# A bias product that reads contiguous columns, with the interleaving moved to the copy out of PSUM

## The chip, the cores and the metric

The kernel runs on one core of a Trainium2 chip. Its engines are TensorE (PE, with its weight loads shown as PEld), VectorE (DVE), ScalarE (ACT), GpSimd (POOL) and SyncE (SP, which issues most DMAs). The metric is the device time of one execution in microseconds; a smaller one is better. The time before is the median of three runs. A difference of under about 1% is hard to tell from no change.

## The reference

Attention over 4 batches, 8 heads, 576 positions and a head size of 64, with a learned bias that depends on the two positions, is followed by a mixture of 8 experts with one expert per token. All is in float32.

```python
scores = scale * np.matmul(q, k.transpose(0, 1, 3, 2))
psi_rel = np.log1p(np.abs(rel))
psi_i = np.log1p(np.maximum(pos[:, None].astype(np.float32), 1.0))
x = (psi_rel / psi_i)[..., None]
h = np.maximum(x @ w1 + b1, 0.0)          # 32 hidden units
bias = h @ w2                              # [576, 576, 8 heads]
scores = scores + bias.transpose(2, 0, 1)[None]
scores = scores - np.max(scores, axis=-1, keepdims=True)
attn = np.exp(scores)
attn = attn / (np.sum(attn, axis=-1, keepdims=True) + 1e-09)
out = np.matmul(attn, v)
...
# tokens [2304, 512]: softmax gate of the best of 8 experts, then
out[mask] = gate_w[mask, None] * (np.maximum(x[mask] @ w1[e], 0.0) @ w2[e])
```

## The kernel before

**Attention.** The work is cut into 80 units. A unit is one head of one pair of batches and one chunk of query rows: chunk c (0 to 3) holds the rows 4p + c with p up to 127, chunk 4 the last 64 rows. The first 40 units belong to the first pair of batches, in the chunk order 4, 0, 1, 2, 3; the second pair repeats the order. A unit (`unit`) runs on PE the scores `s` (L686), on DVE the sum of scores and bias with its minimum (L700), on ACT the exponential (L703), on PE the transposes (L717) into the banks `t0`, `t1` and `m`, on ACT or DVE their copies `pts` (L723), on PE the product with the values (L738) and a last transpose (L743), and on DVE the division (L755).

**The bias.** It is the same for both pairs of batches, so `bias_step` makes it once, in 36 steps (four for chunk 4, eight for each other chunk), between the units of the first pair; most steps have a priority some 13 units ahead of their chunk's first unit. A step covers 16 query rows for all 576 key columns. DVE (seldom POOL or ACT) makes four tiles `hid` of 128 x 576 (L616), each of them 4 rows times 32 hidden units; POOL makes the weights `wt` (L596). PE then multiplies each `hid` by 32 weight columns, and the four products lie side by side in the four column tiles of the array. They go to PSUM in two halves: columns 0 to 255, then columns 256 to 575. Both halves use the one bank `m`, apart from the first steps, which also use `t0`, `t1` and `o`. ACT (seldom DVE) adds a constant and copies each half to the tile `stg` (L644, L648), in pieces of 256, 256 and 64 columns; POOL copies 64 columns to the front (L653) and issues the DMA of `stg` to DRAM (L654). A unit later loads its bias with SP (`bt`, L667).

In `stg`, the first 512 key columns stand in the order c, r (all columns 4r, then all 4r + 1, and so on), since keys are loaded that way. Before the change the product makes this order: PE reads `hid` in steps of four columns (16 bytes), writes the bank in a row, and the copy has both sides contiguous in runs of 64:

```python
... hx[x]()[:, a:a + 256].rearrange("p (r c) -> p c r", c=4) ...   # L629, in steps of 4
... hx[x]()[:, a + 256:a + n] ...                                  # L631, columns 512 to 575
src = m()[:, lo:lo + k].rearrange("p (c r) -> p c r", c=4)         # L640
```

Each float32 product is two instructions in the trace (two passes over its columns), so a step has 16 of 256 columns and 8 of 64.

**The order.** All of attention is given as operations with dependencies, buffers and a priority to a list scheduler (`Sched`) that runs when the program is built and writes every engine's program in one fixed order. Its durations (300 and 440 for the two halves of a product) and the priorities (`oB`, `oO`, `oL`, `BL`, `FINQ`, `WP` and others, in units) are numbers at the head of the file. On the chip each engine goes through its own list in order and waits for semaphores. SP and POOL queue their DMAs in that order too. The tile `hid` has five buffers, `stg` two, `bt` four, `wt` four.

After attention the tokens are sorted to slots by expert and the experts' products run (`moe`); the change doesn't touch that code.

Of the kernel before, what the change touches and what calls it, by code (L numbers as in the profile page):

```python
# [19 lines left out]
B, H, S, D = 4, 8, 576, 64  # L20
# [13 lines left out]
QPE = ((0, 4, 0),)  # L34
EA, EB = 6, 4
NB = NS - EA
PEN, PENP, PACE = 155.677, 2000, 2000
oS, oB, oP, oT, oE, oA, oO, oX, oL = 0.26, -1, -0.817, -0.323, -1, 3.114, -2.843, 1.206, 0.169
BL, BS, QL = 13.245, 0.415, 0.625
FINP, FINQ = 12, 1.278  # L40
FINE, GEP = 1.277, 1
WP, W2P, W1P = 56.805, 56, 70.081
WHP, RLP, XEP, XP = 96.779, 0, -75.386, 5
L1P = [(k, x, r) for k in range(4) for x, r in ((0, 0), (0, 1), (1, 0))]
GL, W0P, W0S = 6.297, -25.544, 4.236
# [210 lines left out]
class Kern:  # L256
# [327 lines left out]
    def bias_step(self, c, g, prio):  # L584

        nc, S = self.nc, self.S
        t0 = c * 32 + g * 4
        tag = ("bias", c, g)
        relu = (c, g) in BACT
        if relu:  # L590

            wts, w = [], lambda x: self.w2bd
        else:
            wt = self.buf("wt", [128, 4, 32], pool="sm_wt")
            wts, w = [wt], lambda x: wt()[:, x]
            S.op([("POOL", 361, lambda: nc.gpsimd.tensor_tensor(wt(), self.w2bd.unsqueeze(1).to_broadcast([128, 4, 32]), self.sall[:, t0 // 4].unsqueeze(2).to_broadcast([128, 4, 32]), ALU.mult))], [], [tag + ("w",)], [wt], prio)  # L596
        hids, hx = [], []
        for x in range(4):
            src, off = (self.L, 499 - 16 * (4 * g + x) - c) if c < 4 else (self.L2, 60 - 4 * (4 * g + x))
            own = BHID.get((c, g))  # L600
            if own is None:
                hid = self.buf("hid", [128, S_])
                hids.append(hid)
            else:

                if x % 2 == 0:
                    big = self.buf("pp", [128, 2 * S_]) if own == "pp" else self.buf("pts", [128, 9, 128], pool="pt")
                    hids.append(big)
                if own == "pp":
                    hid = lambda big=big, x=x: big()[:, S_ * (x % 2):S_ * (x % 2) + S_]  # L610
                else:
                    hid = lambda big=big, x=x: big().rearrange("p a b -> p (a b)")[:, S_ * (x % 2):S_ * (x % 2) + S_]
            hx.append(hid)

            def act(e, hid=hid, src=src, off=off, x=x):
                e.tensor_scalar(hid(), src[:, off:off + S_], self.thr[:, t0 + x:t0 + x + 1], None, ALU.max)  # L616

            def rel(hid=hid, src=src, off=off, x=x):
                nc.scalar.activation(hid(), src[:, off:off + S_], AF.Relu, bias=self.wcol[:, 1:2], scale=self.sall.rearrange("p g t -> p (g t)")[:, t0 + x:t0 + x + 1])

            alts = [("ACT", 667, rel)] if relu else [("DVE", 440, lambda act=act: act(nc.vector)), ("POOL", 1699, lambda act=act: act(nc.gpsimd), PENP)]
            S.op(alts, ["L"] if c < 4 else [], [tag + ("h", x)], [hids[-1]], prio)
        stg = self.buf("stg", [128, 640])
        for k, (a, n) in enumerate(((0, 256), (256, 320))):
            m = self.buf(("t0", "t1", "o", "m")[(2 * g + k) % 4] if c == 4 or c == 0 and g < BBK else "m", [128, 512])

            def mm(a=a, n=n, m=m):
                for x in range(4):
                    nc.tensor.matmul(m()[32 * x:32 * x + 32, 0:256], w(x), hx[x]()[:, a:a + 256].rearrange("p (r c) -> p c r", c=4), start=True, stop=True, tile_position=(0, 32 * x))  # L629
                for x in range(4 if n > 256 else 0):  # L630
                    nc.tensor.matmul(m()[32 * x:32 * x + 32, 256:n], w(x), hx[x]()[:, a + 256:a + n], start=True, stop=True, tile_position=(0, 32 * x))  # L631

            tm = tag + ("m", a)
            S.op([("PE", 300 if n == 256 else 440, mm)], [tag + ("w",)] + [tag + ("h", x) for x in range(4)], [tm], [*wts, m] + hids, prio)

            def ev(e, lo, k, m=m, a=a):
                col = a + lo
                if col < 512:
                    out = stg()[:, 64:576].rearrange("p (c r) -> p c r", c=4)[:, :, col // 4:(col + k) // 4]
                    src = m()[:, lo:lo + k].rearrange("p (c r) -> p c r", c=4)  # L640
                else:
                    out, src = stg()[:, col + 64:col + 64 + k], m()[:, lo:lo + k]
                if e is nc.scalar:
                    e.activation(out, src, AF.Identity, bias=0.0 if relu else self.corr)  # L644
                elif relu:
                    e.tensor_copy(out, src)
                else:
                    e.tensor_scalar(out, src, self.corr, None, ALU.add)  # L648

            for lo, k in ((0, 256), (256, 64))[0:1 if n == 256 else 2]:  # L650
                S.op([("ACT", 144 + 0.833 * k, lambda ev=ev, lo=lo, k=k: ev(nc.scalar, lo, k)), ("DVE", 70 + 1.04 * k, lambda ev=ev, lo=lo, k=k: ev(nc.vector, lo, k), PEN)], [tm] + ([] if relu else ["corr"]), [tag + ("s", lo + a)], [m, stg], prio)
        rows = self.bsc[c].rearrange("i h k -> (i h) k")
        S.op([("POOL", 333, lambda: nc.gpsimd.tensor_copy(stg()[:, 0:64], stg()[:, 576:640]))], [tag + ("s", 512)], [tag + ("t",)], [stg], prio)  # L653
        S.op([("POOL", 1038, lambda: nc.gpsimd.dma_start(rows[128 * g:128 * g + 128, :], stg()))] + ([("SP", 550, lambda: nc.sync.dma_start(rows[128 * g:128 * g + 128, :], stg()), PSB)] if c == 4 or c == 0 else []), [tag + ("t",), tag + ("s", 0), tag + ("s", 256)], [("bsc", c)], [stg], prio, 910)  # L654
# [806 lines left out]
```

## Time and profile before

| | before |
|---|---|
| median of 3 runs | 734.16 us (732.21 to 737.54) |
| the profiled execution | 733.53 us, of which the profile's span is 731.6 us |
| PE busy in the span | 652.0 us (89%) |
| DVE, ACT, POOL busy | 558.2, 466.3, 175.5 us |
| mean granted TensorE clock | 0.97 |
| attention with bias steps | to about 210 us of the span |
| attention without them | 210 to about 410 us |

The profile is one execution. Busy times are unions of the intervals in which the engine had an instruction in flight, so a busy PE includes the tails of its pipeline. The 1.9 us between the span and the execution's time lie outside the profile.

### The profile page before, as it was taken

To read this page: it belongs to the slowest core of one execution; us is meant where nothing else is said; L and a number is where in the kernel's file an instruction comes from. 1 tells how busy PE (TensorE), PEld (TensorE's weight loads), DVE (VectorE), ACT (ScalarE), POOL (GpSimd) and SP (SyncE) were. 2 spreads that over 40 slices of the span, in tenths; PEclk is the share of its full clock that TensorE was granted. 3 is DMA by queue.
4 is the path that set the end of the run, shared out by engine and by line. 5 is a ranking of instruction groups with operands and counts; after the bars stand their busy time and mean duration, and the time that the engine had idled before them with its cause. 6 is when DMAs were issued, how large, how long until landed. Compare 5 with 4: busy or idle time off the path is not lost.

```text
span 731.6 us, 19239 instructions
## 1 busy us (share of the span) xinstructions
PE 652.0 (89%) x6649; PEld 424.6 (58%) x6649; DVE 558.2 (76%) x1579; ACT 466.3 (64%) x1058; POOL 175.5 (24%) x273
## 2 busy tenths in 40 slices
PE   8679999998999979899999965899999998899983
PEld 3345545555467657677776754764674476357541
DVE  5877677788868998898988864869589967978642
ACT  4566567666678888898998434857266546736200
POOL 3545543344221122311201165000000000000163
PEclk9799999999999999999999989999999999999997
DMA  7685544726478966988878669846299459739532
GB/s 233 195 216 173 161 154 135 210 87 164 139 203 196 275 154 129 182 179 201 198 162 188 149 188 215 204 88 186 82 231 191 163 109 222 180 113 188 110 127 99
DMA packets 147908, 124.03 MB, mean 170 GB/s; under 512 B 93830, under 2 KB 122758, under 8 KB 147808
## 3 DMA queue, kind: packets, MB, share of 16 engines
q1 hardware_dynamic: 140400, 97.19, 56.2%
q0 software_dynamic: 7408, 25.52, 10.6%
q8 instruction: 60, 0.98, 0.6%
q14 instruction: 40, 0.33, 0.1%
HBM read 80.70 MB, written 22.29 MB: 141 GB/s over the span
## 4 chain that ended last, share of the span: by engine, by line
issue 37%; PE 27%; DVE 7%; ACT 5%; POOL 4%; DMA 2%; another core or an unknown queue 0%; POOLq 0%; ACTq 0%; DVEq 0%; SPq 0%
PE o L738 8%; PE s L686 6%; PE t L717 5%; PE m L629 4%; ACT pp L703 2%; POOL out L1295 2%; DVE ss L700 2%; DMA mht<-macc 2%; PE o L743 1%; ACT pts L723 1%; PE m L717 1%; DVE khl L513 1%; PE e L1040 1%; DVE pts L723 0%
## 5 line engine op out<-in xcount | busy, mean ns | idle before, releaser
L1290 PE MATMUL p<-w1s,mxt 128*128 (+1 forms) x960 | 126.8, 275 | 4.9 <-DVE macc L1051 3.5
L1290 PE MATMUL p<-w2s,mht 128*128 (+1 forms) x504 | 115.0, 379 | 9.4 <-DVE macc L1382 8.2
L703 ACT ACTIVATE pp<-ss,mx 128x576 f32<-128x576 f32 x144 | 112.7, 787 | 13.5 <-DVE mx L700 12.4
L700 DVE CUSTOM_DVE_ANT_0 ss<-s,bt 128x576 f32<-128x576 f32 x144 | 104.3, 751 | 13.2 <-PE s L686 11.0
L1290 PEld LDWEIGHTS <-mxt 128*128 128x128 f16 (+1 forms) x960 | 93.5, 99 | 31.0 <-issue 4.2
L738 PE MATMUL o<-pts,v 128*64 128x128 f32 x1600 | 105.3, 278 | 2.2 <-DVE xt L755 1.3
L738 PEld LDWEIGHTS o<-pts,v 128*64 128x64 f32 x1600 | 86.1, 136 | 25.5 <-issue 12.9
L1290 PEld LDWEIGHTS <-mht 128*128 128x128 f16 (+1 forms) x504 | 49.0, 99 | 67.5 <-issue 15.2
L616 DVE TENSOR_SCALAR hid<-L,thr 128x576 f32<-128x576 f32 x128 | 65.0, 567 | 29.6 <-PE m L631 29.6
L717 PE MATMUL t<-ident,pp 128*128 128x128 f32 x576 | 85.0, 279 | 2.1 <-ACT pp L703 1.6
L686 PE MATMUL s<-kt,qt 64*128 64x512 f16 (+3 forms) x960 | 75.7, 287 | 4.2 <-DVE mx L700 3.2
L1295 POOL DMA_INDIRECT out<-macc,kept x21 | 21.0, 998 | 239.4 <-DVE macc L1382 235.1
L723 ACT COPY pts<-t 128x512 f32<-128x512 f32 x125 | 70.0, 594 | 11.0 <-PE t L717 9.8
L629 PE MATMUL m<-hid,wt 128*32 128x256 f32 x488 | 68.5, 625 | 8.9 <-ACT stg L644 3.4
L1251 ACT ACTIVATE junk<-raw 128x1024 bf16<-128x1024 f32 x50 | 53.0, 1059 | 31.6 <-DMA raw<-in_moe_w 18.8
L717 PEld LDWEIGHTS t<-ident,pp 128*128 128x128 f32 x576 | 63.8, 141 | 13.1 <-ACT pp L703 4.7
L1344 ACT ACTIVATE h<-p 128x256 f16<-128x256 f32 x78 | 28.5, 384 | 61.9 <-PE p L1290 34.4
L686 PEld LDWEIGHTS <-qt 64*128 64x128 f16 (+1 forms) x960 | 39.3, 97 | 43.9 <-issue 15.5
L644 ACT ACTIVATE stg<-m,corr 128x256 f32<-128x256 f32 (+1 forms) x88 | 33.7, 418 | 46.3 <-PE m L631 24.7
L1382 DVE SCALAR_TENSOR_TENSOR macc<-p,aux,macc 128x512 f32<-128x512 f32 x63 | 46.2, 752 | 21.1 <-PE p L1290 16.1
L1345 DVE SCALAR_TENSOR_TENSOR h<-p,h 128x256 f16<-128x256 f32 x80 | 32.4, 420 | 26.2 <-ACT h L1344 26.2
L1257 DVE SCALAR_TENSOR_TENSOR w1s<-raw,wz,w1s 128x1024 f16<-128x1024 f32 x32 | 40.7, 1278 | 0.1
(335 smaller groups left out, 1063.1 us busy)
## 6 DMA issues: line engine op xcount, KB each, us to landing
raw<-in_moe_w SPq DMA_DIRECT2D x60, 512.0 KB, 4.8
bt<-bsc SPq DMA_DIRECT2D x64, 320.0 KB, 3.5
bsc<-stg POOLq DMA_DIRECT2D x33, 320.0 KB
bt<-bsc SPq DMA_DIRECT2D x32, 160.0 KB, 4.2
xs<-row POOLq DMA_DIRECT2D x16, 256.5 KB
v<-in_v SPq DMA_DIRECT2D x8, 512.0 KB, 5.3
kr<-in_k SPq DMA_DIRECT2D x8, 512.0 KB, 7.8
q<-in_q SPq DMA_DIRECT2D x8, 512.0 KB, 5.5
```

The costliest lines, as they stand in the source:

```text
L616: e.tensor_scalar(hid(), src[:, off:off + S_], self.thr[:, t0 + x:t0 + x + 1], None, ALU.max)
L629: nc.tensor.matmul(m()[32 * x:32 * x + 32, 0:256], w(x), hx[x]()[:, a:a + 256].rearrange("p (r c) -> p c r", c=4), start=True, stop=True, ...
L686: nc.tensor.matmul(out, lq, k, start=xq + xk == 0, stop=xq == 1, tile_position=(64 * b, 0 if c < 4 else 64 * b))
L700: nc.vector.tensor_tensor_reduce(out=sx(), in0=ss[b]()[:, 448 * b:448 * b + S_], in1=bt()[:, 64 - 64 * b:640 - 64 * b], scale=1.0, scalar= ...
L703: nc.scalar.activation(pp()[:, S_ * b:S_ * b + S_], sx(), AF.Exp, bias=mx()[:, b:b + 1], scale=-1.0, accum_out=sums()[:, h, b:b + 1])
L717: nc.tensor.transpose(t()[:, 128 * k:128 * k + 128], pp()[:, lo + 128 * k:lo + 128 * k + 128], self.ident)
L723: (e.copy if e is nc.scalar else e.tensor_copy)(pts()[:, at:at + n].rearrange("p a b -> p (a b)"), t()[:, 0:128 * n])
L738: nc.tensor.matmul(ob()[64 * b:64 * b + 64, k:k + 128], vv[:, 8 + b if j == 4 else 4 * b + j, :], pts()[:, pb, :], start=j == 0, stop=j == ...
L1251: S.op([("ACT", 1230, lambda: nc.scalar.activation(out() if not own else dst(0), rv() if own else raw(), AF.Square, scale=2.0 ** (-8 if wh ...
L1257: S.op([("DVE", 1280, lambda: nc.vector.scalar_tensor_tensor(dst(1), rv(), z(3), dst(0), ALU.mult, ALU.subtract))], [t + (3,), t + (2,)] + ...
L1290: nc.tensor.matmul(out[c, 0:n], lhs[:, c], w[:, bass.ds(ev[s] + at, n)], start=start, stop=stop)
L1382: S.op([("DVE", 750, lambda a=a, r=r, p2=p2: v.scalar_tensor_tensor(a, p2(), r, a, ALU.mult, ALU.add))], [("p2", q, s), ("rs", q)], [("acc ...
```

## The change

The product reads each `hid` in contiguous columns, the first half 256 and the second half all 320 in one matmul, so L631 and its eight instructions a step go. The bank `m` then holds the columns in their natural order, and the copy of each piece of 256 reads PSUM in steps of four elements and writes `stg` in the same runs of 64 as before. The last 64 columns are copied as before. The scheduler's duration of the second half goes from 440 to 390, and numbers that set the order are changed (a table of numbers; its effect on the order is shown behind the diff).

```diff
--- before.py
+++ after.py
@@ -34,12 +34,12 @@
 QPE = ((0, 4, 0),)
 EA, EB = 6, 4
 NB = NS - EA
-PEN, PENP, PACE = 155.677, 2000, 2000
-oS, oB, oP, oT, oE, oA, oO, oX, oL = 0.26, -1, -0.817, -0.323, -1, 3.114, -2.843, 1.206, 0.169
-BL, BS, QL = 13.245, 0.415, 0.625
-FINP, FINQ = 12, 1.278
+PEN, PENP, PACE = 155.677, 2000, 1643.511
+oS, oB, oP, oT, oE, oA, oO, oX, oL = 0.26, -1.529, -0.817, -0.323, -1, 3.114, -3.254, 1.206, 1.584
+BL, BS, QL = 13.929, 0.415, 0.625
+FINP, FINQ = 12, 1.913
 FINE, GEP = 1.277, 1
-WP, W2P, W1P = 56.805, 56, 70.081
+WP, W2P, W1P = 55.887, 56, 70.081
 WHP, RLP, XEP, XP = 96.779, 0, -75.386, 5
 L1P = [(k, x, r) for k in range(4) for x, r in ((0, 0), (0, 1), (1, 0))]
 GL, W0P, W0S = 6.297, -25.544, 4.236
@@ -626,18 +626,16 @@
 
             def mm(a=a, n=n, m=m):
                 for x in range(4):
-                    nc.tensor.matmul(m()[32 * x:32 * x + 32, 0:256], w(x), hx[x]()[:, a:a + 256].rearrange("p (r c) -> p c r", c=4), start=True, stop=True, tile_position=(0, 32 * x))
-                for x in range(4 if n > 256 else 0):
-                    nc.tensor.matmul(m()[32 * x:32 * x + 32, 256:n], w(x), hx[x]()[:, a + 256:a + n], start=True, stop=True, tile_position=(0, 32 * x))
+                    nc.tensor.matmul(m()[32 * x:32 * x + 32, 0:n], w(x), hx[x]()[:, a:a + n], start=True, stop=True, tile_position=(0, 32 * x))
 
             tm = tag + ("m", a)
-            S.op([("PE", 300 if n == 256 else 440, mm)], [tag + ("w",)] + [tag + ("h", x) for x in range(4)], [tm], [*wts, m] + hids, prio)
+            S.op([("PE", 300 if n == 256 else 390, mm)], [tag + ("w",)] + [tag + ("h", x) for x in range(4)], [tm], [*wts, m] + hids, prio)
 
             def ev(e, lo, k, m=m, a=a):
                 col = a + lo
                 if col < 512:
                     out = stg()[:, 64:576].rearrange("p (c r) -> p c r", c=4)[:, :, col // 4:(col + k) // 4]
-                    src = m()[:, lo:lo + k].rearrange("p (c r) -> p c r", c=4)
+                    src = m()[:, lo:lo + k].rearrange("p (r c) -> p c r", c=4)
                 else:
                     out, src = stg()[:, col + 64:col + 64 + k], m()[:, lo:lo + k]
                 if e is nc.scalar:
```

On PE the first bias steps (chunk 4, at the start of the kernel) stand like this before; `o`, `m` and `t` are PSUM banks, `pp`, `pts` and `hid` hold the hidden units, `w2bd` and `wt` are weights, and each row is the four column tiles of one product:

```order
L629 MATMUL o<-pp,w2bd 32x256 x4
L629 MATMUL m<-pp,w2bd 32x256 x4
L631 MATMUL m<-pp,w2bd 32x64 x4
L629 MATMUL t_284<-hid,wt 32x256 x4
L629 MATMUL t_290<-hid,wt 32x256 x4
L631 MATMUL t_290<-hid,wt 32x64 x4
L382 MATMUL m<-bcst 128x1
L629 MATMUL t_318<-pts,wt 32x256 x4
```

and now:

```order
L629 MATMUL o<-pp,w2bd 32x256 x4
L629 MATMUL m<-pp,w2bd 32x320 x4
L629 MATMUL t_280<-hid,wt 32x256 x4
L629 MATMUL t_288<-hid,wt 32x320 x4
L382 MATMUL m<-bcst 128x1
L629 MATMUL t_310<-pts,wt 32x256 x4
```

Every product of 256 and the one of 64 behind it became one of 320; the sequence of the steps is the same.

On ACT one unit in the middle of the stretch with bias steps stands like this before (L644 copies the bias, L703 is the exponential, L742 a small copy for L743, L723 the transposed probabilities):

```order
L703 ACTIVATE pp,sums<-ss,mx 128x576
L742 COPY os<-o 128x128
L644 ACTIVATE stg<-m,corr 128x4x64
L644 ACTIVATE stg<-m,corr 128x64
L723 COPY pts<-t_1860 128x512
L723 COPY pts<-t_1872 128x512
L723 COPY pts<-m 128x128
L703 ACTIVATE pp,sums<-ss,mx 128x576
L644 ACTIVATE stg<-m,corr 128x4x64
```

and now, with line numbers lower by two:

```order
L701 ACTIVATE pp,sums<-ss,mx 128x576
L740 COPY os<-o 128x128
L642 ACTIVATE stg<-m,corr 128x4x64
L642 ACTIVATE stg<-m,corr 128x64
L721 COPY pts<-t_1863 128x512
L721 COPY pts<-t_1877 128x512
L721 COPY pts<-m 128x128
L701 ACTIVATE pp,sums<-ss,mx 128x576
L642 ACTIVATE stg<-m,corr 128x4x64
```

The order within the unit is the same.

On SP, which issues the loads, the part at the first units stands like this before (`bt` is the bias of a unit, read back from the DRAM tile `bsc`; `v`, `q`, `qm`, `kr` are the inputs):

```order
L542 DMA qm<-in_q 64x4x64 x2
L440 DMA v<-in_v 128x4x256
L667 DMA bt<-bsc_197 64x640 x2
L443 DMA v<-in_v 64x4x64
L440 DMA v<-in_v 128x4x256
L324 DMA rcst<-in_rcst 128x293
L325 DMA row<-in_moe_expert_emb 8x512
L667 DMA bt<-bsc_197 64x640 x4
L544 DMA q<-in_q 128x4x256
L582 DMA_TRANSPOSE qt<-qab 128x8x128
L667 DMA bt<-bsc_197 64x640 x2
```

and now:

```order
L542 DMA qm<-in_q 64x4x64 x2
L665 DMA bt<-bsc_197 64x640 x2
L440 DMA v<-in_v 128x4x256
L665 DMA bt<-bsc_197 64x640 x2
L324 DMA rcst<-in_rcst 128x293
L325 DMA row<-in_moe_expert_emb 8x512
L665 DMA bt<-bsc_197 64x640
L443 DMA v<-in_v 64x4x64
L440 DMA v<-in_v 128x4x256
L582 DMA_TRANSPOSE qt<-qab 128x8x128
L665 DMA bt<-bsc_197 64x640 x3
```

Ahead of the second large load of `v` there are now five loads of `bt`, where there were two, and the first load of `q` stands behind the next three instead of ahead of them.

## Rows read from the trace of the kernel before

**Rows 1.** The page: busy time of each engine with its share of the span and its instruction count, and the granted TensorE clock in 40 equal slices of the span (9 is 90% or more of full speed).

```profile
PE 652.0 (89%) x6649; PEld 424.6 (58%) x6649; DVE 558.2 (76%) x1579; ACT 466.3 (64%) x1058; POOL 175.5 (24%) x273
...
PEclk9799999999999999999999989999999999999997
```

**Rows 2.** Busy time by stretch: the stretch in us, its length, then the busy time of PE, PEld, DVE, ACT and POOL (in brackets the instructions), the granted TensorE clock, the share of the DMA engines and GB/s.

```profile
0.00:30.00 30.00, 21.00 (x158) 9.71 (x159) 21.02 (x52) 15.56 (x25) 14.23 (x27) 0.84 0.61 193
30.00:50.00 20.00, 17.15 (x172) 9.06 (x169) 16.15 (x40) 10.58 (x20) 8.85 (x20) 0.90 0.83 242
50.00:60.00 10.00, 8.36 (x99) 4.92 (x96) 8.02 (x24) 8.66 (x21) 6.00 (x9) 1.00 0.80 191
60.00:80.00 20.00, 20.00 (x252) 11.66 (x250) 13.78 (x34) 11.66 (x28) 9.08 (x17) 1.00 0.51 154
80.00:110.00 30.00, 27.23 (x315) 13.85 (x311) 21.55 (x60) 18.73 (x51) 14.57 (x26) 1.00 0.53 170
110.00:170.00 60.00, 58.26 (x677) 33.39 (x673) 44.90 (x115) 42.07 (x116) 25.02 (x43) 1.00 0.48 144
170.00:190.00 20.00, 17.34 (x206) 8.68 (x204) 15.55 (x50) 12.81 (x34) 7.95 (x15) 1.00 0.57 153
190.00:210.00 20.00, 19.98 (x245) 11.93 (x242) 13.34 (x41) 13.66 (x38) 3.54 (x7) 1.00 0.78 195
210.00:410.00 200.00, 186.70 (x2397) 143.02 (x2396) 174.80 (x608) 176.19 (x453) 41.03 (x64) 1.00 0.81 184
```

**Rows 3.** The chain that ended last, in order of time, over one unit of attention and the start of the next: start in us, length in us, engine, tile, line.

```profile
119.75 1.09 PE m L629 x8
120.83 1.24 PE o L738 x20
122.08 1.02 PE m L629 x8
123.10 0.12 PE m L631 x8
123.21 0.58 PE t L717 x4
123.80 0.11 PE o L743
...
124.45 0.84 PE s L686 x12
125.31 1.09 PE m L629 x8
```

**Rows 4.** The timeline of PE in narrow windows between 208.1 and 209.4 us, one half of a bias step at full clock: start, length from the first start to the last end, line, operands, count. A window lists what was in flight in it, so each row of four is one pass of four column tiles.

```profile
208.14 0.64 PE L629 MATMUL m<-hid,wt 128*32 128x256 f32 x4
208.58 0.65 PE L629 MATMUL m<-hid,wt 128*32 128x256 f32 x4
209.03 0.26 PE L631 MATMUL m<-hid,wt 128*32 128x64 f32 x4
209.10 0.24 PE L631 MATMUL m<-hid,wt 128*32 128x64 f32 x4
209.27 0.33 PE L717 MATMUL t<-ident,pp 128*128 128x128 f32 x1
```

**Rows 5.** The same for a bias step on tiles t at 27.8 to 29.9 us: first the row of the busy time by stretch (length, PE busy, granted clock, DMA share, GB/s), then three passes of the timeline.

```profile
27.90:29.90 2.00, 2.00 (x24) 0.50 0.42 114
...
29.19 0.65 PE L629 MATMUL t<-pp,wt 128*32 128x256 f32 x4
29.64 0.30 PE L631 MATMUL t<-pp,wt 128*32 128x64 f32 x4
...
29.72 0.33 PE L631 MATMUL t<-pp,wt 128*32 128x64 f32 x4
```

**Rows 6.** The timeline of DVE and ACT in the unit of rows 3: start, length, line, operands, count, and in square brackets the idle time before with what ended it.

```profile
123.23 1.95 DVE L616 TENSOR_SCALAR hid<-L,thr 128x576 f32<-128x576 f32 x4 [0.78 <-PE m L631]
123.36 0.68 ACT L644 ACTIVATE stg<-m,corr 128x256 f32<-128x256 f32 x2 [0.95 <-PE m L631]
...
123.93 1.07 ACT L723 COPY pts<-t 128x512 f32<-128x512 f32 x2
...
125.03 0.82 ACT L703 ACTIVATE pp<-ss,mx 128x576 f32<-128x576 f32 x1
...
126.59 0.47 ACT L644 ACTIVATE stg<-m,corr 128x256 f32<-128x256 f32 x1 [0.65 <-POOL qs L560]
...
126.97 0.76 ACT L703 ACTIVATE pp<-ss,mx 128x576 f32<-128x576 f32 x1
...
127.72 0.25 ACT L742 COPY os<-o 128x128 f32<-128x128 f32 x1
...
128.93 0.68 ACT L644 ACTIVATE stg<-m,corr 128x256 f32<-128x256 f32 x2 [0.95 <-PE m L631]
```

**Rows 7.** Groups of instructions from 50 to 210 us, each shape apart: line, engine, operation, operands, shapes, count, then busy time in us, mean ns of one, and the idle time before them with what ended it.

```profile
L644 ACT ACTIVATE stg<-m,corr 128x256 f32<-128x256 f32 x55 | 26.1, 475 | 42.9 <-PE m L631 22.0 <-issue 8.8 <-PE m L629 6.9
...
L644 ACT ACTIVATE stg<-m,corr 128x64 f32<-128x64 f32 x28 | 8.6, 307 | 0.0
...
L616 DVE TENSOR_SCALAR hid<-L,thr 128x576 f32<-128x576 f32 x111 | 55.9, 562 | 28.4 <-PE m L631 28.4
...
L629 PE MATMUL m<-hid,wt 128*32 128x256 f32 x448 | 61.3, 625 | 7.6 <-ACT pts L723 3.3 <-ACT stg L644 3.2 <-DVE lgs L862 0.5
```

## The prediction

> **What bounds the kernel now.** I read the page first: PE is busy for 89% of the span [rows 1]. Where a busy engine is also the one waited for differs by stage, so the busy time by stretch comes next. The steps of the bias lie before 210 us. In the 100 us made of 60 to 80, 110 to 170 and 190 to 210, PE is busy for 97 to 100% and DVE and ACT for 58 to 75%; in the 60 us between them (50 to 60, 80 to 110, 170 to 190) PE has 84 to 91% and DVE 72 to 80% [rows 2]. Behind 210 us ACT and DVE have 88 and 87%, so a faster PE gives nothing there.
>
> The chain that ended last then shows what PE does. From 119.75 to 125.31 us it stays on PE without a wait: half a bias step, the product with the values, the other half, transposes, scores, and the next unit's half step [rows 3]. That is 5.56 us for one unit and one bias step. Of it the bias has 1.09 us at the start and 1.13 from 122.08 to 123.21.
>
> What holds up the bias product is in the narrow windows. A pass of four column tiles with 256 columns starts at 208.14, the next at 208.58, the passes of 64 columns at 209.03 and 209.10, the transposes at 209.27 [rows 4]. So 256 columns in steps of four cost 0.44 to 0.45 us a pass, 1.7 ns a column, and 64 contiguous ones 0.07, 1.1 ns a column. [...] Four contiguous streams side by side do run faster per column, which the 64 columns show.
>
> **The change part by part.** *The product.* I need a contiguous pass of 256 and of 320 columns, which the trace lacks. One side: 64 columns in 0.07 to 0.08 us, so 1.25 ns a column at most, 0.32 and 0.40 us. Other side: a float32 transpose, a single tile, reads 128 contiguous columns in 0.11 us [rows 3], 0.86 ns a column, 0.22 and 0.275 us. With 0.86 ns the 64 columns would be 0.055 and leave some 0.015 for starting four tiles; this fits both rows, and I take 0.24 and 0.29 us. First half: two passes, 0.89 before (208.14 to 209.03), 0.48 after, 0.41 saved. Second half: 0.89 and 0.14 for the passes of 64, 1.03 before, 0.58 after, 0.45 saved. The switch to the transposes (209.10 to 209.27) stays. Together 0.86 us a step; by the bounds 0.48 (1.28 and 1.60 us for the four passes become 0.64 and 0.80) to 0.93.
>
> *Where it counts.* From 50 to 210 us there are 448 instructions of 256 columns [rows 7], 16 a step, so 28 steps; three more from 30 to 50 and five before. In the 100 us where PE is full I count 100 / 5.56 = 18 steps at the full 0.86: 15.5 us. The other 10 stand where PE waits for 9 to 16% of the time and DVE is nearly level; I take half, 4.3 us, and half for the three from 30 to 50, 1.3. The first five I count at nothing: they hide behind loads and DVE, PE being busy for 21 of the first 30 us [rows 2]; without that cover they would give 4.3. Sum: 21.1 us.
>
> *What is late next.* The unit would take 5.56 - 0.86 = 4.70 us. DVE starts the four hidden tiles when the second half's product has ended (123.23, waiting for PE) and needs 1.95 us, until 125.18; the next product starts at 125.31 [rows 3, 6]. DVE idles 28.4 us in front of these tiles from 50 to 210 us, all of it waiting for PE's product [rows 7]. This loop is level with PE's own work in between, and the same 0.86 us go out of it, so it allows 4.70 too, but no less. ACT goes through copies and exponentials in a fixed list and waits 0.65 us before its copy at 126.59 (put down to POOL, though it copies what PE has just written) and 0.95 before that at 128.93 [rows 6], so it works for 3.96 of the 5.56 us and would have 0.74 left. POOL (0.42 of the time from 110 to 170) and the DMA engines (0.48) have room [rows 2].
>
> *The copy.* It now reads PSUM in steps of four. No row shows such a read. The copy of 256 takes 475 ns and that of 64 307 [rows 7], so 0.875 ns an element and 0.25 us fixed. One bound is no cost. For the other I take the factor of two that reading in steps costs PE per column (1.7 against 0.86 ns): 0.22 us more a copy, 0.44 a unit, which leaves ACT 0.3 of its 0.74 us. Nothing faster is in sight, since contiguous runs are read now. I take half of it; hidden in the full units, but the places with less slack pay: 1 us off. The last 64 columns and the writes to `stg` stay as they are.
>
> [...]
>
> *The order.* The list of the first units on SP and the units on ACT keep their sequence but for a few places. Five loads of bias, not two, now stand ahead of the second load of the values; should they wait for a free `bt` buffer, the loads behind them on SP wait too, and the product with the values of the next heads waits for those. That is worth up to one unit, 5.6 us; the cover is that 50 to 60 us is a stretch in which PE works at 84%. The other way, an order that suits a shorter product can take out some of the waits that remain (PE idles 8.8 of the 160 us from 50 to 210 [rows 2]). The moved priorities of the weights' loads (`WP`) come to a unit at most and lie behind 210 us. I take nothing, with +6 and -6 as bounds. Behind 210 us I take nothing either: the work and its bound are the same.
>
> *Sum.* 21.1 - 1 = 20 us off the profiled execution's 733.5 us: 713.5. The median of the runs is 0.6 us above that execution, so 714.
>
> **The rivals.** *ACT or DVE takes over.* The unit comes down to 5.15 us only, since engines that work through a fixed list with 0.3 us to spare pick up waits from each other; 28 x 0.41 = 11 us, 722. For it: the loop over the hidden tiles has no slack at all, and the copies may take longer. Against it: behind 210 us ACT runs at 88% without harm to the unit.
>
> *The full gain.* All 36 steps save 0.86 (31 us) or the order removes other waits: 703. For it: PE is what the chain shows. Against it: DVE's 70 to 80% in the weaker stretches.
>
> *The product doesn't get faster.* Four different streams could be limited by their sum and not by the steps. Then nothing moves, 734. Against it stands the pass of 64 columns; it would need 0.11 us at the pace of the 256.
>
> *Slower: the copies in steps take the bound.* Two copies a unit are on ACT, with PE, which needs the bank `m` again, behind them. ACT works 3.96 us a unit; it exceeds the old 5.56 us once a copy of 256 costs 0.8 us more, 1.28 in place of 0.475. At 5 ns an element it would be 1.53 us, the unit 6.07, and 28 x 0.5 = 14 us more: 747. Nothing in the rows comes near such a price; it is the one operation that I can't see.
>
> **How the numbers follow.** The forecast (706 to 719) has 0.62, the takeover 0.17, the full gain 0.09, no effect (the product as before, or an order that costs what the product gives) 0.08, slower 0.04. The range, 702 to 726, takes in the forecast, the takeover and most of the full gain, and leaves out some 0.15. A measurement here tells about 1%, 7 us, from no change. Faster by more than that: 0.62 + 0.17 + 0.09 less 0.01 for a takeover that leaves under 7 us = 0.87; within it 0.09; slower 0.04.
>
> **What the profile of the changed kernel would show.** L629 alone, with passes of 256 contiguous columns starting 0.22 to 0.26 us apart and of 320 0.27 to 0.32. A unit between 110 and 140 us of 4.7 to 4.8 us in the chain, still on PE. The last bias step near 190 us in place of 209. The copy of 256 at 475 to 700 ns. About 200 us from there to the end of attention, as now. I would be wrong if the passes kept 0.44 us, if the copies took over 1 us, or if the unit stayed over 5 us with ACT or DVE in the chain.

## The result, and the profile after

| | before | after |
|---|---|---|
| median of 4 runs each | 734.18 us (732.21 to 737.54) | 710.74 us (708.46 to 711.39) |
| ratio | | 0.966 (95% interval 0.962 to 0.970) |
| profiled execution, its span | 733.53, 731.6 us | 711.31, 709.4 us |
| last scores matmul starts at | 412.4 us | 385.9 us |
| from there to the end of the span | 319.2 us | 323.5 us |

The kernel is 3.4% faster. By the profile attention ends 26.5 us earlier, and 4.3 us of that are lost again behind it. In line numbers those of after are lower by two from L629 on: L642 is the copy to `stg`, L684 the scores, L715 the transposes, L736 the product with the values.

The page of after, busy time and granted clock (as [rows 1]):

```profile
PE 627.2 (88%) x6361; PEld 415.9 (59%) x6361; DVE 559.0 (79%) x1580; ACT 465.0 (66%) x1057; POOL 174.6 (25%) x274
...
PEclk9799999999999999999999877999999999999997
```

PE loses 24.8 us of work, and the other engines keep theirs. Its busy time by stretch, with the columns of [rows 2]:

```profile
50.00:60.00 10.00, 9.43 (x117) 5.79 (x111) 9.36 (x27) 8.66 (x21) 5.79 (x9) 1.00 1.11 209
60.00:80.00 20.00, 18.37 (x238) 10.96 (x234) 16.12 (x40) 11.23 (x30) 11.88 (x21) 1.00 0.71 236
80.00:110.00 30.00, 28.41 (x335) 16.60 (x328) 28.33 (x74) 24.35 (x64) 15.57 (x26) 1.00 0.48 135
110.00:170.00 60.00, 56.21 (x676) 34.26 (x674) 51.01 (x142) 47.73 (x131) 28.24 (x51) 0.97 0.63 186
170.00:180.00 10.00, 8.78 (x115) 5.08 (x115) 9.09 (x30) 7.39 (x21) 1.75 (x5) 1.00 0.62 192
180.00:385.00 205.00, 192.86 (x2473) 147.31 (x2465) 176.91 (x620) 181.53 (x470) 42.02 (x66) 1.00 0.81 188
```

From 80 to 110 us DVE is now as busy as PE, and from 110 to 170 PE still leads. The chain that ended last, over one unit there (as [rows 3]):

```profile
116.33 0.64 PE m L629 x8
116.97 1.24 PE o L736 x20
118.22 0.67 PE m L629 x8
118.89 0.59 PE t L715 x4
119.48 0.11 PE o L741
...
120.13 0.84 PE s L684 x12
...
120.99 0.64 PE m L629 x8
```

The two halves of a bias step hold 0.64 and 0.67 us of the chain, where they held 1.09 and 1.13 [rows 3], and the unit takes 4.66 us in place of 5.56. Nothing else in it changed: scores 0.84, values 1.24. PE is still what the chain follows. Its timeline in narrow windows shows the passes (as [rows 4]; of the second pass one instruction starts at 116.55, the other three at 116.58):

```profile
116.33 0.42 PE L629 MATMUL m<-hid,wt 128*32 128x256 f32 x4
116.55 0.42 PE L629 MATMUL m<-hid,wt 128*32 128x256 f32 x4
...
118.14 0.48 PE L629 MATMUL m<-hid,wt 128*32 128x320 f32 x4
118.44 0.45 PE L629 MATMUL m<-hid,wt 128*32 128x320 f32 x4
```

So 256 contiguous columns take 0.24 us a pass and 320 take 0.29. The groups from 50 to 210 us, each shape apart (as [rows 7]):

```profile
L616 DVE TENSOR_SCALAR hid<-L,thr 128x576 f32<-128x576 f32 x107 | 54.5, 568 | 8.9 <-PE m L629 8.4
...
L642 ACT ACTIVATE stg<-m,corr 128x256 f32<-128x256 f32 x53 | 25.1, 473 | 20.1 <-PE m L629 15.2 <-issue 3.9 <-POOL qs L560 0.4
...
L629 PE MATMUL m<-hid,wt 128*32 128x320 f32 x224 | 20.9, 445 | 3.3 <-ACT stg L642 3.2
L629 PE MATMUL m<-hid,wt 128*32 128x256 f32 x216 | 18.0, 389 | 1.9 <-ACT pts L721 1.5
```

The product with the bank `m` costs 38.9 us there in place of the 61.3 of the strided 256 columns alone [rows 7]. The copy that now steps through PSUM takes 473 ns; it took 475. DVE waits 8.9 us in front of the hidden tiles in place of 28.4.

### The profile page after: what moved, and what is told of

The parts are those of the page before. It is cut to its first block, busy times and chain, and to the rows that moved or that the text cites. A ratio compares the mean times of both kernels' runs of the same rounds, so it can differ in the third digit from the quotient of the medians.

```text
span 709.4 us, 18648 instructions
## 1 busy us (share of the span) xinstructions
PE 627.2 (88%) x6361; PEld 415.9 (59%) x6361; DVE 559.0 (79%) x1580; ACT 465.0 (66%) x1057; POOL 174.6 (25%) x274
## 4 chain that ended last, share of the span: by engine, by line
issue 38%; PE 34%; DVE 7%; ACT 6%; DMA 6%; POOL 5%; SPq 1%; POOLq 0%; ACTq 0%; DVEq 0%
PE o L736 11%; PE t L715 7%; PE s L684 7%; PE m L629 5%; ACT pp L701 3%; POOL out L1293 3%; DMA macc<-xs,kept 2%; DVE ss L698 2%; DVE khl L513 1%; ACT pts L721 1%; PE o L741 1%; POOL macc L1302 1%; DMA bsc<-stg 1%; PE m L715 1%; DMA raw<-in_moe_w 1%
## 5 line engine op out<-in xcount | busy, mean ns | idle before, releaser
L736 PE MATMUL o<-pts,v 128*64 128x128 f32 x1600 | 107.6, 282 | 1.7 <-DVE xt L753 1.0
L736 PEld LDWEIGHTS o<-pts,v 128*64 128x64 f32 x1600 | 88.5, 139 | 18.5 <-issue 8.8
L715 PE MATMUL t<-ident,pp 128*128 128x128 f32 x576 | 86.0, 280 | 2.3 <-ACT pp L701 1.7
L684 PE MATMUL s<-kt,qt 64*128 64x512 f16 (+3 forms) x960 | 75.4, 285 | 4.2 <-DVE mx L698 3.3
L715 PEld LDWEIGHTS t<-ident,pp 128*128 128x128 f32 x576 | 63.0, 140 | 18.5 <-issue 10.1
L684 PEld LDWEIGHTS <-qt 64*128 64x128 f16 (+1 forms) x960 | 38.9, 97 | 47.0 <-issue 18.5
L629 PE MATMUL m<-hid,wt 128*32 128x320 f32 (+1 forms) x488 | 44.9, 417 | 9.3 <-ACT stg L642 3.2
L642 ACT ACTIVATE stg<-m,corr 128x256 f32<-128x256 f32 (+1 forms) x88 | 33.6, 416 | 22.6 <-PE m L629 17.6
```

Of the source, the lines that this page charges most:

```text
L629: nc.tensor.matmul(m()[32 * x:32 * x + 32, 0:n], w(x), hx[x]()[:, a:a + n], start=True, stop=True, tile_position=(0, 32 * x))
L684: nc.tensor.matmul(out, lq, k, start=xq + xk == 0, stop=xq == 1, tile_position=(64 * b, 0 if c < 4 else 64 * b))
L715: nc.tensor.transpose(t()[:, 128 * k:128 * k + 128], pp()[:, lo + 128 * k:lo + 128 * k + 128], self.ident)
L736: nc.tensor.matmul(ob()[64 * b:64 * b + 64, k:k + 128], vv[:, 8 + b if j == 4 else 4 * b + j, :], pts()[:, pb, :], start=j == 0, stop=j == ...
```

## The experiments

The series ran on different chips: the kernel before took 734.35 us beside e1 to e4, 724.17 beside g1 to g4 and 723.78 (one execution) beside h1 to h3. Attention in before ends at the same place in its three profiles (last scores at 412.4, 411.9 and 412.1 us), so the 10 us between the first and the last series lie behind it; on the chip of g1 to g4 before was not profiled. So times are compared within a series only, and the times expected of g1, g2 and g4 were set from the first series, in which before takes 10 us more; these three came out 1.5 to 8 us under their ranges.

**Product or order.** e1 has the new product and copy with the old numbers:

```diff
-PEN, PENP, PACE = 155.677, 2000, 1643.511
-oS, oB, oP, oT, oE, oA, oO, oX, oL = 0.26, -1.529, -0.817, -0.323, -1, 3.114, -3.254, 1.206, 1.584
+PEN, PENP, PACE = 155.677, 2000, 2000
+oS, oB, oP, oT, oE, oA, oO, oX, oL = 0.26, -1, -0.817, -0.323, -1, 3.114, -2.843, 1.206, 0.169
...
```

> The product and the copy as after, the numbers that set the order as before. Theory: the gain is the shorter product alone, so 711 to 716 us, within 1% of after, with the last bias step near 182 us of the span. Rival: the order fitted to it gives a good part of the 23 us, then 722 us or more. The first product of a unit in the middle of the first half should stand 4.6 to 4.8 us from the next by the theory, over 5 us by the rival.

Measured: 708.98 us (707.21 to 710.25), a ratio to before of 0.966 (0.963 to 0.970), the same as after's. Units stand 4.66 us apart, and the last bias step ends at 182.0 us. The time lies 2 us under the expected range and within 1% of after: the product alone gives all of the gain.

e2 is the other half: the new numbers with the old product.

```diff
-                    nc.tensor.matmul(m()[32 * x:32 * x + 32, 0:n], w(x), hx[x]()[:, a:a + n], ...)
+                    nc.tensor.matmul(m()[32 * x:32 * x + 32, 0:256], w(x), hx[x]()[:, a:a + 256].rearrange("p (r c) -> p c r", c=4), ...)
...
-                    src = m()[:, lo:lo + k].rearrange("p (r c) -> p c r", c=4)
+                    src = m()[:, lo:lo + k].rearrange("p (c r) -> p c r", c=4)
```

> The product and the copy as before (256 columns in steps of four), the numbers that set the order, the scheduler's 390 for the second half too, as after. Theory: the order takes nothing out by itself, 732 to 740 us, perhaps slower than before since it is planned for a product that is shorter than the real one. Rival: the order carries the gain, under 722 us.

Measured: 738.94 us, ratio 1.006 (1.003 to 1.009). The last scores come at 415.5 us, 3 us later than before. The order gives nothing by itself, and with the long product it costs a little.

**What in the product.** e3 keeps the last 64 columns in a product of their own:

```diff
-                for x in range(4):
-                    nc.tensor.matmul(m()[32 * x:32 * x + 32, 0:n], w(x), hx[x]()[:, a:a + n], ...)
+                for lo, hi in ((0, 256), (256, n))[0:1 if n == 256 else 2]:
+                    for x in range(4):
+                        nc.tensor.matmul(m()[32 * x:32 * x + 32, lo:hi], w(x), hx[x]()[:, a + lo:a + hi], ...)
```

> As after, but the columns 512 to 575 keep a product of their own, now 256 and 64 contiguous columns. Theory: the contiguous reading is the gain, and the two matmuls in one give only the start of the 64 columns: 0.24 + 0.075 us for a pass in place of 0.293, so 0.045 us a step, 28 steps, 1.3 us: 711 to 714 us. Rival: a good part of the gain is the eight instructions fewer and the switch between shapes; then 717 us or more.

Measured: 713.20 us (707.56 to 714.50), ratio 0.970 (0.965 to 0.976); the unit is again 4.66 us. Eight instructions fewer a step are not the gain.

e4 differs from e3 in the step by which the 256 columns are read:

```diff
-                        nc.tensor.matmul(m()[32 * x:32 * x + 32, lo:hi], w(x), hx[x]()[:, a + lo:a + hi], ...)
+                        ... hx[x]()[:, a + lo:a + hi].rearrange("p (r c) -> p c r", c=2) ...
...
-                    src = m()[:, lo:lo + k].rearrange("p (r c) -> p c r", c=4)
+                    src = m()[:, lo:lo + k].rearrange("p (b r a) -> p a b r", b=2, a=2)
```

> As after with the columns 512 to 575 in a product of their own, but the 256 columns are read in steps of two (8 bytes in place of 16), and the copy makes the order from that. Theory one: reading in any step costs what steps of four cost, 0.44 us a pass, so 730 to 736 us. Theory two: only a step that leaves one float in 16 bytes costs; with two floats in each 16 bytes the pass stays at 0.24 us, 711 to 715 us. Between them, if the cost goes with the bytes passed over: some 0.3 us a pass and 715 to 722 us.

Measured: 708.74 us, ratio 0.968 (0.964 to 0.973), 2 us under the range of theory two. Steps of two cost next to nothing. In the groups from 50 to 210 us of e4 an instruction takes 403 ns, in after it takes 389 (the fence above), and in before 625 in steps of four [rows 7]:

```profile
L630 PE MATMUL m<-hid,wt 128*32 128x256 f32 x440 | 37.4, 403 | 6.3 <-ACT stg L643 4.2 <-ACT pts L722 1.5
```

By their starts the passes of e4 are 0.252 us apart (median), those of after 0.240, those of before 0.439. g2 goes the other way, to steps of eight:

```diff
-                        ... hx[x]()[:, a + lo:a + hi].rearrange("p (r c) -> p c r", c=2) ...
+                        ... hx[x]()[:, a + lo:a + hi].rearrange("p (r c) -> p c r", c=8) ...
...
-                    src = m()[:, lo:lo + k].rearrange("p (b r a) -> p a b r", b=2, a=2)
+                    src = m()[:, lo:lo + k].rearrange("p (h c r) -> p c r h", h=2, c=4)
```

> As after, with the columns 512 to 575 in a product of their own, but the 256 columns are read in steps of eight (32 bytes); the copy makes the order from that. Theory one: every read that finds one float in its 16 bytes costs the same, so a pass takes 0.44 us as in steps of four, and the kernel 730 to 740 us. Theory two: the cost goes with the bytes passed over, so 0.85 us a pass; each of 28 steps is then 1.6 us longer than before, 775 us or more.

Measured: 728.44 us (726.01 to 731.53), ratio 1.006 (1.002 to 1.009), just that of e2, which has the same order and steps of four. The same group in g2:

```profile
L631 PE MATMUL m<-hid,wt 128*32 128x256 f32 x448 | 62.7, 633 | 6.3 <-ACT stg L644 3.2 <-ACT pts L723 2.7
```

Passes stand 0.446 us apart. So the price doesn't go with the bytes passed over: 0.446 us for steps of 32 bytes, 0.439 for 16. Steps of 4 and 8 bytes run at one pace (0.240 and 0.252 us) and steps of 16 and 32 at another. That is as theory two of e4 and theory one of g2 have it. The four sizes show that the pace changes between 8 and 16 bytes; what makes it change there was not shown.

**The first steps.** g1 gives the four steps of chunk 4 their old product:

```diff
+                old = c == 4
+                for lo, hi in ((0, 256), (256, n))[0:2 if old and n > 256 else 1]:
...
+                        nc.tensor.matmul(..., cols.rearrange("p (r c) -> p c r", c=4) if old and lo == 0 else cols, ...)
...
```

> As after, but the four steps of chunk 4, the first ones of the kernel, read their 256 columns in steps of four and have the 64 columns in a product of their own, as before. Theory: the chain of the start runs through these steps (their copies, the two tiles stg, the writes of stg to DRAM), so they are worth 2 to 4.5 us: 712.5 to 715 us, and the transpose of the key scales (L489), at 17.6 us in after and 19.6 in before, comes at 19 us or later. Rival, as the prediction had it: they hide behind loads and DVE, so 711 us within 1 us and that transpose at 17.6.

Measured: 704.37 us (700.33 to 708.11) where the kernel after, in the same series (g4, below), took 700.22 (696.63 to 700.91). The scores' matmuls of g1, then of g4 (count; shortest, median and longest in ns; first and last start; shapes):

```profile
L688 PE MATMUL s<-kt,qt x960: 188/282/400, 39.5 to 386.9; 64*128 64x512 f16 x77, 64*128 64x64 f16 x76, 64*64 64x64 f16 x20, 64*64 64x512 f16 x19
```

```profile
L684 PE MATMUL s<-kt,qt x960: 188/282/400, 36.3 to 383.4; 64*128 64x512 f16 x77, 64*128 64x64 f16 x76, 64*64 64x64 f16 x20, 64*64 64x512 f16 x19
```

The first scores come at 39.5 us in place of 36.3, the last at 386.9 in place of 383.4. One execution of each doesn't fix the size: the first scores of after stand at 37.2, 36.3 and 37.1 us in its three profiles and its last ones at 385.9, 383.4 and 387.1, so g1's last scores lie within that spread. Its first scores don't: they are 2.3 to 3.2 us later than those of after and level with those of before (39.4 to 40.1). So the four steps of 0.86 us are worth some 2 to 3 us, most of their length. ACT's timeline shows the link, first in before, then in after (in square brackets the idle time before and what ended it):

```profile
18.94 0.38 ACT L644 ACTIVATE stg<-m 128x256 f32<-128x256 f32 x1 [4.08 <-DMA bsc<-stg]
```

```profile
16.90 0.38 ACT L642 ACTIVATE stg<-m 128x256 f32<-128x256 f32 x1 [4.05 <-DMA bsc<-stg]
```

`stg` has two buffers. This copy needs one that a DMA is still writing to DRAM, and the write could start only when the first products were done. Behind the copy comes the bank `m`, and with it the transpose of the key scales, in before, after and g1:

```profile
19.64 0.27 PE L489 MATMUL m<-ident,kz 128*4 128x128 f32 x1 [2.21 <-DVE stg L646]
```

```profile
17.60 0.27 PE L489 MATMUL m<-ident,kz 128*4 128x128 f32 x1 [3.54 <-DVE stg L644]
```

```profile
19.86 0.27 PE L489 MATMUL m<-ident,kz 128*4 128x128 f32 x1 [2.38 <-DVE stg L648]
```

From it come the keys and the first scores.

**What binds next.** g3 halves each product and leaves out the other half of the bias:

```diff
-                    nc.tensor.matmul(m()[32 * x:32 * x + 32, 0:n], w(x), hx[x]()[:, a:a + n], ...)
+                    nc.tensor.matmul(m()[32 * x:32 * x + 32, 0:n // 2], w(x), hx[x]()[:, a:a + n // 2], ...)
...
+                    src = m()[:, 0:128].rearrange("p (r c) -> p c r", c=4).unsqueeze(2).to_broadcast([128, 4, 2, 32])
...
```

> As after, but each product reads half of its columns, 128 and 160; the other half is left out and the copies, of the same size as in after, repeat what there is, so half of the bias is another one. It asks what binds the units next. Passes of 0.13 and 0.16 us, 0.5 us less a step. Theory: PE still binds the full units, so the unit comes from 4.65 to 4.15 us, and the end of attention 8 to 12 us earlier than in after. Rival: DVE's hidden tiles or ACT bind now; the unit stays at 4.5 us or more and attention gains under 4 us.

Measured: 693.50 us against 700.22 of after; last scores at 376.2 us, 7.2 earlier. Neither case has it whole. The scores of the 14th unit start 0.6 us later than in after, so up to there (112 us of before) the shorter product gave nothing more; the granted clock was also lower there, here from 30 to 50 us in after (g4, below) and then in g3:

```profile
30.00:50.00 20.00, 15.51 (x169) 8.23 (x162) 17.72 (x47) 13.79 (x30) 10.67 (x24) 1.00 0.88 230
```

```profile
30.00:50.00 20.00, 15.68 (x129) 8.57 (x128) 15.63 (x39) 10.82 (x22) 9.69 (x21) 0.66 0.72 200
```

From the 14th to the 30th unit 7.0 us come out. The chain of g3 in that stretch:

```profile
116.38 0.41 PE m L629 x8
...
118.03 0.84 PE s L684 x12
...
118.89 0.43 PE m L629 x8
...
120.56 0.41 PE m L629 x8
```

From one half (116.38) to the same half of the next step (120.56) the unit is 4.18 us, still on PE. Busy time of g3 from 110 to 170 us:

```profile
110.00:170.00 60.00, 54.54 (x753) 36.72 (x754) 57.45 (x162) 52.63 (x146) 28.71 (x53) 1.00 0.72 207
```

DVE has 96%, more than PE, so the hidden tiles on DVE are likely to bind next; that no run shows. Which of the lower clock and DVE held the first 13 units was not told apart.

**Behind attention.** h1 and h2 are the kernel before, h3 is after, all on one chip.

> The kernel before, a second profile. In the profile of before the stretch from the last scores to the end lasted 319.3 us, in that of after 323.6. Theory: this stretch, whose code is the same in both, spreads by some us between executions, so the profiles of before taken here differ from each other or from that of after by no rule: the mean of the two is within 2 us of the one of after on the same chip. Rival: the change lengthens it by 3 to 5 us, so both are that much shorter than after's.

> The kernel after, a third profile, on the chip of the two of before that go with it. Theory: from the last scores to the end within 2 us of the mean of those two. Rival: 3 to 5 us longer than both. The last scores should stand 25 to 28 us ahead of before's by both.

> The kernel before, a third profile, on the same chip: it shows how far two executions of one kernel differ behind the last scores. Theory: by 1 to 5 us; rival: by less than 1 us, with after's 3 to 5 us longer.

The scores' matmuls of h1, h2 and h3 (count; shortest, median and longest in ns; first and last start):

```profile
core 0 of [0], span 722.9 us
...
L686 PE MATMUL s<-kt,qt x960: 188/282/401, 40.1 to 411.9; 64*128 64x512 f16 x77, 64*128 64x64 f16 x76, 64*64 64x64 f16 x20, 64*64 64x512 f16 x19
```

```profile
core 0 of [0], span 722.7 us
...
L686 PE MATMUL s<-kt,qt x960: 188/282/400, 39.7 to 412.1; 64*128 64x512 f16 x77, 64*128 64x64 f16 x76, 64*64 64x64 f16 x20, 64*64 64x512 f16 x19
```

```profile
core 0 of [0], span 701.9 us
...
L684 PE MATMUL s<-kt,qt x960: 188/282/401, 37.1 to 387.1; 64*128 64x512 f16 x77, 64*128 64x64 f16 x76, 64*64 64x64 f16 x20, 64*64 64x512 f16 x19
```

From the last scores to the end these leave 311.0 and 310.6 us for before and 314.8 for after. (One execution each: 724.70, 724.45 and 703.78 us.) The two of before agree within 0.4 us and after is 4 us longer, as in the first pair: that is the rival, not the theory of a mere spread. Three executions can't refute the spread, though: on the chip of g1 to g4 before took from 719.08 to 729.84 us in 17 executions. The kernel after a second time, beside g1 to g3:

> The kernel after itself, a second time. Theory: what was lost behind attention (27 us ahead of before at the last scores, 22 at the end) is spread between executions of the expert stage, so the lead at the last scores is again 26 to 27 us, but the stretch from there to the end differs by over 1 us from the first time. Rival: it belongs to the change, and the lead at the end is 22 us within 0.5 again. The time 708 to 713 us.

Measured: 700.22 us, ratio 0.965 (0.960 to 0.971); 383.4 us to the last scores and 315.5 behind them. Before was not profiled on that chip, so the second number tells little alone. The first shows that the lead at the last scores spreads too: 29.0 us against the 412.4 of before here, 26.5 in the first pair, 24.9 in h3 against h1 and h2 (25 to 28 were expected there).

But the loss isn't tied to the change in a simple way either:

| one chip | last scores | from there to the end |
|---|---|---|
| e2 (new order, old product) | 415.5 us | 324.5 us |
| e1 (old order, new product) | 384.8 | 322.8 |
| e3 (new order, 256 and 64 columns) | 388.9 | 322.4 |
| e4 (new order, steps of two) | 388.1 | 318.3 |

| another chip | last scores | from there to the end |
|---|---|---|
| g4 (after) | 383.4 us | 315.5 us |
| g1 (after with the first four steps as before) | 386.9 | 311.6 |
| g2 (new order, steps of eight) | 413.9 | 311.5 |
| g3 (half product) | 376.2 | 311.4 |

e3 and e4 reach the last scores within 0.8 us of each other and differ by 4.1 us behind it; g1 and g4 by 3.9. Each row is one execution, and some are far from their median: those of g1 and g3 were the fastest of six and of four (700.33 us with a median of 704.37, 689.50 with 693.50), that of e2 the slowest of five (741.77 with 738.94). So 4 us in these tables can be the spread of one kernel. The difference between before and after arises early, in the stretch in which the experts' first weights and the gathered tokens come in: the first copy of the second weights to `wx` on DVE stands 67.0 us behind the last scores in after and 63.0 in before, 63.5 in h3 and 60.0 and 58.7 in h1 and h2. There the DMA engines are nearly full in three of the four rows below while DVE and ACT stand some half idle, here in before, then in after (columns as in [rows 2]; the share of the DMA engines is the last but one):

```profile
442.00:452.00 10.00, 6.09 (x43) 4.37 (x42) 5.29 (x8) 5.05 (x9) 7.58 (x8) 0.93 1.05 181
452.00:462.00 10.00, 6.57 (x62) 5.36 (x62) 6.03 (x14) 4.71 (x8) 2.09 (x3) 0.83 1.08 223
```

```profile
416.00:426.00 10.00, 8.31 (x40) 5.64 (x40) 6.01 (x12) 5.46 (x9) 7.23 (x7) 0.56 1.03 271
426.00:436.00 10.00, 4.34 (x34) 3.34 (x33) 3.12 (x11) 3.30 (x6) 3.78 (x4) 0.61 0.79 276
```

Which transfer comes late in after was not found, and no run changed that stage alone. The granted clock differs too, 0.56 and 0.61 in after against 0.93 and 0.83, and no run tells the two apart. It stays open.

## Why the prediction was right, and where its terms were off

The time (711 us for 714 forecast), the sign and the mechanism came out as forecast: PE's passes get shorter, and the full units get shorter by that. That the total is so near is in part luck, since two terms put at nothing were wrong in opposite directions. By its steps, with the lead of after over before read at the scores of single units in the first pair of profiles:

- **The product: right.** 0.24 and 0.29 us a pass were forecast and measured (0.240 and 0.293 by the median of the starts from 50 to 210 us). A step saves 0.91 us in the chain (1.09 + 1.13 against 0.64 + 0.67), 0.86 forecast. The pace of the contiguous 64 columns and of the transposes [rows 3, 4] was the right neighbour. The 0.08 us in its slower bound is the distance from 29.64 to 29.72 in [rows 5].
- **Where it counts, from 60 to 210 us: right.** 15.5 + 4.3 = 19.8 us forecast; the lead grows from 5.0 us at the fifth unit (60.1 us in before) to 25.3 at the 30th (210.6), 20.3 us. If the 18 full steps gave 0.91 us each (16.4 us), 0.39 is left for each of the ten others, close to the half that they were counted at; this is a division and not a measurement.
- **The first five steps at nothing: wrong.** The step that failed is "they hide behind loads and DVE", taken from PE's busy time in the first 30 us [rows 2]. A PE that is idle for a third of a stretch can still stand in the chain that sets its end: the lead is 2.2 us at the first scores already (37.2 against 39.4), and g1 gives it back, by way of the two tiles `stg` and their write to DRAM. Only the fifth step, which runs at a granted clock of 0.50 in both kernels, is rightly at nothing, though for another reason than cover (last section).
- **Three steps from 30 to 50 us at half, 1.3 us: too little in the first pair, not settled.** From the first scores to the fifth unit the lead grows from 2.2 to 5.0 us. In e1, g4 and h3, against the same profile of before, it grows by 1.1, 3.1 and 1.6, so the term may well be right. What part of it the product has, and what part the order and loads, was not told apart.
- **The copy: 1 us too much.** From the bank `m` 473 ns against 475 for ACT over the whole run, 483 against 484 for the three copies on DVE. The upper bound carried PE's factor of two over to another engine and another memory.
- **The order at nothing: right** by e1 and e2. The last bias step ends at 180.5 us, 28.8 earlier, where near 190 was expected. Most of that is the lead, since e1, with the old list, ends it at 182.0; the new list has the last six steps one unit earlier.
- **Behind attention at nothing: wrong by 4.3 us**, for a cause that is open. One pair of profiles gives the 4.3 us; by the medians the whole gain is 23.4 us. The loss offsets most of what the start gave, so the total is nearer than its parts, which is luck: 5.0 + 20.3 + 1.2 (from the 30th unit to the last scores) - 4.3 = 22.2 us of the span, 20 forecast.
- **The rivals.** ACT or DVE taking over at 5.15 us a unit is refuted: 4.66 now, and 4.18 in g3. The loop over the hidden tiles was said to allow no less than 4.70; it does, since the product is itself a part of that loop. Stepped copies that bind are refuted by their 473 ns.

## What to carry to other kernels

Make a rearrangement in the copy out of PSUM rather than in what the matmul reads, or at least read the columns in steps of no more than two floats: the copy cost nothing here (473 ns in steps against 475), a pass in steps of two floats took 0.252 us against 0.240, and in steps of four the matmul lost a factor of 1.8 at full clock (0.439 us). Count such a gain at full where PE stands in the chain, and look for that chain at the start too, where busy times are low: here the two buffers of `stg` tied a short product to a DMA, for which ACT idled 4.08 us in before. After a gain on one engine a stage behind it may hand some of it back, as 4.3 us went here in the first pair for a cause that is open, so compare the lead at the end of each stage and not only the total, and take more than one execution of each kernel before a few us are put down to a cause.

## What the runs showed of the hardware

At half clock the contiguous read is hardly faster than the strided one. In after one bias step runs at a granted clock of 0.50; the row of that stretch, and its four passes in narrow windows:

```profile
25.60:27.80 2.20, 2.20 (x19) 0.65 (x18) 2.20 (x5) 1.23 (x1) 1.36 (x1) 0.50 0.63 159
```

```profile
25.67 0.66 PE L629 MATMUL t<-pp,wt 128*32 128x256 f32 x4
26.10 0.65 PE L629 MATMUL t<-pp,wt 128*32 128x256 f32 x4
...
26.53 0.76 PE L629 MATMUL t<-pp,wt 128*32 128x320 f32 x4
27.06 0.76 PE L629 MATMUL t<-pp,wt 128*32 128x320 f32 x4
```

256 columns take 0.43 us and 320 take 0.53, where full clock gives 0.24 and 0.29. In steps of four they took 0.45 at half clock [rows 5] and 0.44 at full [rows 4]. So the pace of contiguous columns goes with the granted clock, by a factor of 1.8 for both sizes, and that of columns in steps of four doesn't. At a clock of 0.50 the two happen to be nearly level (0.43 and 0.45 us), and nearly all that a pass gains it gains at full clock.
